# Loading the first half of batch 0's queries and keys uncast from two other queues, and taking the strided heads first

## The chip, the cores and the metric

The kernel runs on one core of a Trainium2 chip. The metric is device microseconds (us) from the start to the end of one execution; lower is better. Before the change the median of 3 runs is 304.52 us (304.48 to 304.62).

## What is computed

Attention with two kinds of local masks, then a two-layer MLP with SiLU. There are 8 batches, 8 heads, 576 positions and a head size of 64; the MLP is 512 to 2048 to 512. Heads 0 to 3 see the last 32 positions; heads 4 to 7 see every fourth of the last 128 positions.

```python
scores = scale * np.matmul(q, k.transpose(0, 1, 3, 2))
mask_plain = (rel >= 0) & (rel < window)                                   # window = 32
mask_dil = (rel >= 0) & (rel < window * dilation) & (rel % dilation == 0)  # dilation = 4
attn = softmax(np.where(masks, scores, -1e9))     # masks: plain for heads 0..3, dilated for 4..7
x = (attn @ v).transpose(0, 2, 1, 3).reshape(B * S, H * D)
h = x @ w_in
return (h * (1.0 / (1.0 + np.exp(-h)))) @ w_out
```

All inputs and the output are float32 in DRAM. The kernel works in float16 on chip.

## The kernel before

**Order of the work.** The program is scheduled by hand: the order in which the Python code calls a helper is the order in which each engine's queue gets its instructions. The MLP of batch b runs on TensorE while the attention of later batches is threaded in between its matmuls by a small plan (plan_of). Only batch 0's attention has no MLP to hide behind, so it is cut in two parts and written out by hand (lines 917 to 956): part 0 is positions 0 to 255, part 1 is positions 256 to 575. In the helpers, z = 0 means the plain heads (0 to 3) and z = 1 the strided heads (4 to 7); which = 1 is k and which = 0 is q.

**Loads.** Every load is issued by GpSimd (POOL) and converts float32 to float16 on the way. load_part(which, part) (line 133) loads all 8 heads of one part of batch 0's q or k into rows0, a view of the tile gT, which is free until the MLP starts. Part 0 puts 4 consecutive positions of each head on one of 64 partitions; the DRAM runs are 256 floats (1 KB) and land as 512 bytes. POOL's queue starts with load_part for k and q of part 0 (lines 207 and 208). Then come the identity matrix and the small mask band (lines 209 to 217), then k and q of part 1 (218, 219), the 8 loads of v for batch 0 (220), the first three quarters of w_in (222) and a piece of batch 1's k (224). The trace shows POOL's v loads waiting for earlier loads to land (the wait list puts 1.6 us on k and 1.4 us on q of part 1 ahead of line 183).

**Batch 0, part 0.** transpose0(z, which, part, copy) transposes the 4 heads of one group with TensorE into PSUM (line 302 for the strided heads, 8 transposes; line 313 for the plain heads, 16 transposes), and one engine copies the result to SBUF (line 307 to kC or qC, line 317 to kT or qT). The callers choose that engine: act is ScalarE (ACT), dve is VectorE (DVE). mask0 writes the mask into PSUM with two matmuls (line 435), scores0 adds the scores (line 390 strided, line 374 plain, 32 small matmuls each), max0 takes the row maximum (DVE, line 464), shift0 subtracts it for the strided heads (DVE, line 477), scaled scales it for the plain ones (line 483), and exps runs the exponential: one ACT instruction for the strided heads (line 563), eight with an accumulator for the plain heads (line 574). build_mask_b (line 231) makes the mask's operand on DVE from the identity and the band.

**Part 1 and the MLP.** The same steps follow for part 1, whose k and q copies stand on ACT behind part 0's exponentials. values0 and finish0 make xT, the MLP's input. warm (line 686) puts a few filler matmuls ahead of the MLP. layer1_part (line 754) multiplies w_in with part 0 of batch 0; each quarter of w_in serves 4 of the 16 column blocks (f = 0 to 3, 4 to 7, 8 to 11, 12 to 15). The plan of batch 0 puts part 1's values between them, at f = 8 and f = 10, and behind the first of these POOL's second wave of loads (loads_held, line 824).

```python
    transpose0(1, 1, 0, act)
    build_mask_b()
    transpose0(0, 1, 0, act)
    mask0(1, 0)
    transpose0(1, 0, 0, dve)
    transpose0(0, 0, 0, act)
    scores0(1, 0)
```

Of the kernel before, what the change touches and what calls it, by code (L numbers as in the profile page):

```python
# [9 lines left out]
F32 = mybir.dt.float32  # L10
# [8 lines left out]
DIL = 4  # L19
# [10 lines left out]
def kernel(  # L30
# [9 lines left out]
    nc = tc.nc  # L40
    B, H, S, D = q.shape
# [3 lines left out]
    HH = H // 2  # L45
# [8 lines left out]
    SA = NS // 2  # L54
# [6 lines left out]
    cpool = ctx.enter_context(tc.tile_pool(name="const", bufs=1))  # L61
# [62 lines left out]
    def rows0(which, part):  # L124


        t = gT[:, 4 * which : 4 * which + 4, :].rearrange("p f c -> p (f c)")
        n = H * DIL * D
        return t[0 : (SA, S - SA)[part] // DIL, part * n : part * n + n].rearrange(
            "p (h u d) -> p h u d", h=H, d=D  # L130
        )

    def load_part(which, part):

        nc.gpsimd.dma_start(  # L135
            out=rows0(which, part).rearrange("p h u d -> p h (u d)"),
            in_=bass.AP(
                (q, k)[which].tensor,
                part * SA * D,
                [[DIL * D, (SA, S - SA)[part] // DIL], [S * D, H], [1, DIL * D]],  # L140
            ),
        )

    def load_squares(b, z, which):

        for half in (0, 1):
            for x in (0, 1):  # L150
                o = half * HF + x * QB
                nc.gpsimd.dma_start(  # L152
                    out=qk[b, z, which][o : o + QB],
                    in_=bass.AP(
                        (q, k)[which].tensor,
                        (b * H + z * HH + half * HH // 2) * S * D + x * QB,
                        [[(1 + z) * D, QB], [(1 + z) * QB * D, GN[z]], [1, (QB, GW)[z]]],
                    ),
                )
# [36 lines left out]
    def load_w_out(c):  # L196
# [3 lines left out]
        )  # L200


    eps = cpool.tile([P, 1], F32, name="eps")
    nc.vector.memset(eps, EPS)
    band = cpool.tile([P, KB], F32, name="band")
    nc.vector.memset(band[0:W], 0.0)
    load_part(1, 0)
    load_part(0, 0)
    make_identity(nc, ident)
    nc.gpsimd.affine_select(  # L210
        out=band[0:W], in_=band[0:W], compare_op=ALU.is_ge, fill=NEG,
# [3 lines left out]
        out=band[0:W], in_=band[0:W], compare_op=ALU.is_ge, fill=NEG,  # L215
# [15 lines left out]
    def build_mask_b():  # L231

        nc.vector.tensor_copy(ident4, ident[0:W, None, 0:W].broadcast_to([W, 4, W]))
        nc.vector.tensor_scalar(
            mask_b.rearrange("p t (k x) -> p t k x", x=2),
            band[0:W].rearrange("p (x k) -> p k x", x=2)[:, None].broadcast_to([W, 2, W, 2]),
            1.0 / scale, None, ALU.mult,
        )
        nc.vector.memset(mask_b[:, 0].rearrange("p (k x) -> p k x", x=2)[:, :, 0], NEG / scale)
# [13 lines left out]
    def att(b):  # L253
        if b not in state:
            state[b] = {
                "qT": qTs[b % 2],
                "kT": kTs[b % 2],
                "qC": qCs[b % 2],
                "kC": kCs[b % 2],
                "vw": vws[b % 2],  # L260
                "pt": {},
                "xT": [xtp.tile([P, 2, S], F16, tag=f"xT{z}", name=f"xT_{b}_{z}") for z in (0, 1)],
            }
        return state[b]
# [26 lines left out]
    def transpose0(z, which, part, copy):  # L291

        a = att(0)
        src, t0 = rows0(which, part)[:, z * HH : z * HH + HH], part * SA
        pp = src.shape[0]
        if z:
            t = ps.tile([P, HH, 2, pp], F16, tag="ps", name=f"t{which}_0_{z}_{part}")
            for h in range(HH):  # L300
                for x in (0, 1):
                    nc.tensor.transpose(
                        t[:, h, x], src[:, h, 2 * x : 2 * x + 2].rearrange("p u d -> p (u d)"), ident[0:pp, 0:pp]
                    )
            dst, o = ((a["qC"], 0), (a["kC"], W))[which]
            o += t0 // DIL
            copy(dst[:, :, :, o : o + pp], t)
        else:
            t = ps.tile([P, 2, DIL, pp], F16, tag="ps", name=f"t{which}_0_{z}_{part}")
            for h in (0, 1):  # L310
                for x in range(DIL):
                    for i in (0, 1):
                        nc.tensor.transpose(
                            t[i * HF : i * HF + HF, h, x, :], src[:, 2 * i + h, x, :], ident[0:pp, 0:pp]
                        )
            dst = (a["qT"], a["kT"][:, :, W:])[which][:, :, t0 : t0 + pp * DIL]
            copy(dst.rearrange("d h (p u) -> d h p u", u=DIL), t.rearrange("d h u p -> d h p u"))
# [48 lines left out]
    def score(b, h, j, dst, start=True):  # L366

        if b >= DT[0]:
            score_turned(b, 0, h, 0, j, dst)
            return  # L370
        a = att(b)
        hp, o = (h % 2, h // 2 * D) if b == 0 else (h // 2, (h + h // 2) % 2 * D)
        r = slice(o, o + D)
        nc.tensor.matmul(  # L374
            dst[h * QB : h * QB + QB],
            a["qT"][r, hp, j * QB : j * QB + QB],
            keys(b, a["kT"][r, hp, j * QB : j * QB + KB]),
            start=start,
            stop=True,
            skip_group_check=not start,  # L380
        )

    def score_class(b, h, c, j, dst, start=True):

        if b >= DT[1]:
            score_turned(b, 1, h, c, j, dst)
            return
        a = att(b)
        r = slice(c % 2 * D, c % 2 * D + D)
        nc.tensor.matmul(  # L390
            dst[h * QB : h * QB + QB],
            a["qC"][r, h, c // 2, j * QB : j * QB + QB],
            keys(b, a["kC"][r, h, c // 2, j * QB : j * QB + KB]),
            start=start,
            stop=True,
            skip_group_check=not start,
        )

    def width(b, z, g):

        if b == 0:
            return 8 + g * (4 if z else 2)
        return 10 if z or g else 8
# [37 lines left out]
    def scores0(z, part):  # L441

        n = (2, 3)[part]
        w = width(0, z, part)
        sd = att(0)["s", z, part]
        if z:
            for t in range(n):
                for e in (0, 1):
                    for h in range(HH):
                        for m in (0, 1):  # L450
                            score_class(0, h, 2 * e + m, 2 * part + t, sd[:, m, e * n + t], False)
        else:
            for j in range(w):
                for h in (0, 2, 1, 3):
                    score(0, h, 8 * part + j, sd[:, j], False)
        att(0)["raw", z, part] = sd[:, :, 0 : 2 * n] if z else sd[:, 0:w]

    def max0(z, part):

        w = width(0, z, part)  # L460
        raw = att(0)["raw", z, part]
        nm = att(0)["nm", z, part] = stat.tile([P, WM], F32, tag="nm", name=f"nm_0_{z}_{part}")
        d = nm[:, 0:w].rearrange("p (m t) -> p m t", m=2) if z else nm[:, 0:w]
        nc.vector.tensor_reduce(out=d, in_=raw, axis=AX.X, op=ALU.max, negate=True)
# [135 lines left out]
    def turned(b, z, hi):  # L600

        a = att(b)
        w = width(b, z, hi)
        key = z, hi * (b == 0)
        if key not in a["pt"]:
            a["pt"][key] = ptp.tile([P, DIL * NC, KB], F16, tag="pt", name=f"pt_{b}_{z}_{hi}")
        o = width(b, z, 0) * hi if b else 0
        out = a["pt"][key][:, o : o + w].rearrange("p t c -> p (t c)")
        src = a["pn", z, hi][:, 0:w].rearrange("p t c -> p (t c)")
        if b == 0:  # L610
            out, src = out.bitcast(U32), src.bitcast(U32)
        nc.vector.transpose(out, src)  # L612
# [193 lines left out]
    dve, act = nc.vector.tensor_copy, nc.scalar.copy  # L806
# [106 lines left out]
    def turn0(z, part):  # L913
        normal(0, z, part)
        turned(0, z, part)

    transpose0(1, 1, 0, act)
    build_mask_b()
    transpose0(0, 1, 0, act)
    mask0(1, 0)  # L920
    transpose0(1, 0, 0, dve)
    transpose0(0, 0, 0, act)
    scores0(1, 0)
    max0(1, 0)
    shift0(1, 0)
    exps(0, 1, 0)
# [80 lines left out]
```

## Time and profile before

| | us |
|---|---|
| median of 3 runs | 304.52 |
| the profiled execution, its own time | 305.81 |
| its span, first to last instruction | 303.8 |
| PE (TensorE matmul) busy | 292.5, 96% of the span |
| ACT busy / DVE busy / POOL busy | 203.1 / 192.9 / 118.8 |
| mean granted TensorE clock | 0.999 |

PE is TensorE's matmul row, PEld its weight loads. The chain of waits gives PE 91% of the span, DMA 5%, POOL 1%. From about 30 us on PE hardly pauses; in the first 5.8 us it does nothing. So almost all of the time that is not PE's own lies in the first 28 us, and that is the stretch that the change touches.

In the timeline a row is: start, duration, engine, line, operation, output<-input, count, and in brackets the idle time ahead of it with what ended that idle time. In the table of windows a row is: the stretch, its length, busy time of PE, PEld, DVE, ACT and POOL with the number of instructions, the granted clock, the busy share of the 16 DMA engines (over 1 where packets overlap) and the bytes written in GB/s. Sizes given for a DMA are those that are written: a converting load reads twice as much.

The DMA list gives the two part-0 loads 256.0 KB each with 4.5 us (k) and 5.2 us (q) from issue to landing, the two part-1 loads 320.0 KB with 6.4 and 7.6 us, and the four loads of w_in 512.0 KB with a median of 8.3 us. In this kernel SyncE's queue (SP) issues only the stores of the output, the first of them at 55.3 us; ACT issues no DMA.

### The profile page before, as it was taken

The numbers are of one execution on the slowest core, as the hardware profiler recorded it, in microseconds if no ns is written. First come the engines' busy times: TensorE is split into PE (matmuls) and PEld (weight loads), VectorE is DVE, ScalarE is ACT, GpSimd is POOL, SyncE is SP. The second block draws the span as 40 slices with busy tenths as digits, with TensorE's granted clock in tenths as the row PEclk, the third lists the DMA queues.
The fourth block names the chain that finished last, engine by engine and source line by source line (L and its number), as shares of the span: only waits on it lengthen the run. The fifth ranks groups of instructions, "written<-read, shape, count | busy, mean of one in ns | idle before, by whom it ended". The sixth has DMA issues, their size and how long they took to land.

```text
span 303.8 us, 10280 instructions
## 1 busy us (share of the span) xinstructions
PE 292.5 (96%) x4395; PEld 185.9 (61%) x4395; DVE 192.9 (63%) x357; ACT 203.1 (67%) x683; POOL 118.8 (39%) x182
## 2 busy tenths in 40 slices
PE   2989999999999999999999999999999999999995
PEld 1656754677545774477644775478644775477543
DVE  1895469557997868866893768955893765800012
ACT  3677599775898659965894659976796558246200
POOL 8617326768997295336806086250000000000000
PEclk9999999999999999999999999999999999999999
DMA  8998999999999899399959199390002100210021
GB/s 100 142 196 135 193 205 124 220 154 145 132 163 198 93 71 130 113 111 40 124 72 184 38 60 131 112 121 2 2 37 106 37 2 12 95 37 0 9 97 69
DMA packets 113213, 30.47 MB, mean 100 GB/s; under 512 B 95520, under 2 KB 108688, under 8 KB 113168
## 3 DMA queue, kind: packets, MB, share of 16 engines
q0 software_dynamic: 107840, 20.38, 85.9%
q1 hardware_dynamic: 5328, 9.44, 8.7%
q8 instruction: 34, 0.56, 0.8%
q14 instruction: 11, 0.09, 0.1%
HBM read 40.75 MB, written 9.44 MB: 165 GB/s over the span
## 4 chain that ended last, share of the span: by engine, by line
PE 91%; DMA 5%; POOL 1%; issue 1%; DVE 0%; POOLq 0%
PE o L798 37%; PE h L727 37%; PE h L754 5%; PE o L774 5%; PE x L643 4%; DMA w_in<-in_moe_w_in_dram 3%; DMA gT<-in_q_dram 3%; PE s L364 2%; PE t L283 1%; POOL gT L135 1%; PE s L374 0%; PE ss L364 0%; PE s L390 0%; POOL w_in L191 0%; POOL vw L183 0%
## 5 line engine op out<-in xcount | busy, mean ns | idle before, releaser
L735 ACT ACTIVATE gT<-h 128x576 f16<-128x576 f32 x112 | 72.9, 651 | 63.6 <-PE h L727 63.4
L798 PE MATMUL o<-w_out,gT 128*128 128x512 f16 (+2 forms) x528 | 113.8, 373 | 0.0
L727 PE MATMUL h<-xT,w_in 128*128 128x288 f16 x896 | 113.2, 286 | 0.0
L727 PEld LDWEIGHTS <-w_in 128*128 128x128 f16 x896 | 86.6, 98 | 23.3
L798 PEld LDWEIGHTS <-gT 128*128 128x128 f16 x528 | 50.1, 98 | 56.0
L574 ACT ACTIVATE pe<-ms,nm 128x64 f32<-128x64 f32 x238 | 78.9, 333 | 0.1
L783 DVE COPY ob<-o 128x512 f32<-128x512 f32 (+2 forms) x35 | 23.0, 666 | 51.6 <-PE o L798 50.6
L574 ACT ACTIVATION_READ_ACCUMULATOR pe<-ms,nm 128x1 f32 x238 | 44.5, 187 | 0.0
L152 POOL DMA_DIRECT2D n<-in_k_dram x44 | 31.9, 732 | 26.5 <-DVE kC L337 25.1
L408 DVE SCALAR_TENSOR_TENSOR ms<-s,mask 128x512 f32<-128x512 f32 x28 | 19.2, 686 | 27.5 <-PE s L364 20.9
L152 POOL DMA_DIRECT2D n<-in_q_dram x44 | 31.9, 732 | 4.2 <-DMA n<-in_q_dram 3.5
L174 POOL DMA_DIRECT2D vw<-in_v_dram x32 | 18.3, 578 | 31.3 <-PE x L643 26.5
L596 DVE TENSOR_TENSOR pn<-pe,r 128x640 f16<-128x640 f32 (+2 forms) x32 | 25.3, 792 | 1.1
L183 POOL DMA_DIRECT2D vw<-in_v_dram x32 | 21.2, 667 | 11.5 <-DMA w_out<-in_moe_w_out_dram 8.4
L612 DVE STREAM_TRANSPOSE pt<-pn 128x640 f16<-128x640 f16 (+4 forms) x32 | 24.7, 772 | 1.1
L488 DVE TENSOR_REDUCE nm<-ms 128x10 f32<-128x640 f32 (+1 forms) x28 | 21.9, 786 | 0.9
L754 PE MATMUL h<-xT,w_in 128*128 128x256 f16 (+1 forms) x128 | 18.0, 291 | 1.2 <-DMA w_in<-in_moe_w_in_dram 0.9
L643 PEld LDWEIGHTS <-vw 32*64 32x64 f16 (+1 forms) x1264 | 12.8, 107 | 5.6 <-issue 5.2
L754 PEld LDWEIGHTS <-w_in 128*128 128x128 f16 x128 | 11.9, 99 | 6.0 <-DMA w_in<-in_moe_w_in_dram 2.1
L676 DVE CAST xT<-x 128x288 f16<-128x288 f32 x26 | 10.1, 450 | 8.2 <-PE x L643 8.2
L774 PE MATMUL o<-w_out,gT 128*128 128x512 f16 x64 | 14.7, 380 | 0.0
L643 PE MATMUL x<-pt,vw 32*64 32x64 f16 (+2 forms) x1264 | 14.6, 193 | 0.0
(94 smaller groups left out, 204.2 us busy)
## 6 DMA issues: line engine op xcount, KB each, us to landing
out_dram<-ob SPq DMA_DIRECT2D x35, 256.0 KB, 3.4
n<-in_k_dram POOLq DMA_DIRECT2D x24, 108.0 KB, 4.7
n<-in_q_dram POOLq DMA_DIRECT2D x24, 108.0 KB, 4.5
vw<-in_v_dram POOLq DMA_DIRECT2D x31, 80.0 KB, 3.9
vw<-in_v_dram POOLq DMA_DIRECT2D x32, 72.0 KB, 4.0
w_in<-in_moe_w_in_dram POOLq DMA_DIRECT2D x4, 512.0 KB, 8.3
w_out<-in_moe_w_out_dram POOLq DMA_DIRECT2D x4, 512.0 KB, 14.4
n<-in_k_dram POOLq DMA_DIRECT2D x20, 72.0 KB, 4.5
```

The costliest lines, as they stand in the source:

```text
L152: nc.gpsimd.dma_start(out=qk[b, z, which][o : o + QB], in_=bass.AP((q, k)[which].tensor, (b * H + z * HH + half * HH // 2) * S * D + x * Q ...
L488: nc.vector.tensor_reduce(out=nm[:, 0:w], in_=ms[:, 0:w], axis=AX.X, op=ALU.max, negate=True)
L574: nc.scalar.activation(pe[:, t, :], src[t], AF.Exp, bias=a["nm", z, hi][:, t : t + 1], scale=k, accum_out=l[:, t : t + 1],)
L596: nc.vector.tensor_tensor(pn[:, 0:w], a["pe", z, hi][:, 0:w], r[:, 0:w, None].broadcast_to([P, w, KB]), ALU.mult)
L612: nc.vector.transpose(out, src)
L643: nc.tensor.matmul(x[h // 2][h % 2 * D : h % 2 * D + D, col : col + wd], vws[b % 2][r, NB + kb * DIL + c if z else kb], turned_cols(b, pt[ ...
L727: nc.tensor.matmul(h[:, half, 0:HS], w_in16[:, c, f * P : f * P + P], xT[c // 2][:, c % 2, half * HS : half * HS + HS], start=(c == cs[0]) ...
L735: nc.scalar.activation(gT[:, f, s0 : s0 + S].rearrange("p (a c) -> p a c", a=2), h[:, :, 0:HS], AF.Silu)
L754: nc.tensor.matmul(hs[i // m][:, i % m, 0 : c1 - c0], w_in16[:, c, (f + i) * P : (f + i + 1) * P], xT[c // 2][:, c % 2, c0:c1], start=(c = ...
L774: nc.tensor.matmul(o, gT[:, f, t * P : (t + 1) * P], w_out16[:, f, :], start=(f == 0), stop=(f == NFF - 1),)
L783: copy(ob, o)
L798: nc.tensor.matmul(o[:, 0, 0:m], gT[:, f, t * P : (t + 1) * P], w_out16[:, f, cols], start=(f == 0), stop=(f == NFF - 1),)
```

## The change

The part-0 loads leave POOL. Four new float32 tiles (64 partitions, 4 heads, 256 floats: 256 KB each) take the uncast rows of k and q, one for each head group. SP issues k, ACT issues q, the strided heads' tile first on both. The conversion to float16 into rows0 becomes four engine instructions of 64x1024 elements: DVE converts k, ACT converts q. Then the hand-written order of part 0 changes: build_mask_b goes to the front; the strided k and q are converted and transposed, and their scores are taken ahead of the transposes of the plain q; the copy of the plain k goes from ACT to DVE. DVE's queue is now: mask, cast of the strided k, cast of the plain k, copy to qC, copy to kT. ACT's queue is: two DMA issues, cast of the strided q, copy to kC, cast of the plain q, copy to qT.

```diff
+    stage = {
+        (z, which): cpool.tile([SA // DIL, HH, DIL * D], F32, name=f"stage{z}{which}")
+        for z in (1, 0) for which in (1, 0)
+    }
+    def load_stage(z, which):
+        (nc.scalar, nc.sync)[which].dma_start(
+            out=stage[z, which],
+            in_=bass.AP(
+                (q, k)[which].tensor,
+                z * HH * S * D,
+                [[DIL * D, SA // DIL], [S * D, HH], [1, DIL * D]],
+            ),
+        )
+    def cast_stage(z, which, copy):
+        copy(
+            rows0(which, 0)[:, z * HH : z * HH + HH].rearrange("p h u d -> p h (u d)"), stage[z, which]
+        )
...
+    for z in (1, 0):
+        for which in (1, 0):
+            load_stage(z, which)
     eps = cpool.tile([P, 1], F32, name="eps")
...
-    load_part(1, 0)
-    load_part(0, 0)
     make_identity(nc, ident)
...
+    build_mask_b()
+    cast_stage(1, 1, dve)
+    cast_stage(1, 0, act)
     transpose0(1, 1, 0, act)
-    build_mask_b()
-    transpose0(0, 1, 0, act)
+    cast_stage(0, 1, dve)
     mask0(1, 0)
     transpose0(1, 0, 0, dve)
+    cast_stage(0, 0, act)
+    transpose0(0, 1, 0, dve)
+    scores0(1, 0)
     transpose0(0, 0, 0, act)
-    scores0(1, 0)
     max0(1, 0)
```

## The prediction, made before the change was run

> **What bounds the kernel now.** I read the chain of waits in order of time first. Up to 22 us its long pieces are transfers:
>
> ```profile
> 4.49 7.63 DMA gT<-in_q_dram
> 12.12 0.28 issue
> 12.41 0.66 POOL vw L183
> 13.07 0.75 POOL w_in L191
> 13.82 8.20 DMA w_in<-in_moe_w_in_dram
> 22.02 0.05 issue
> 22.06 1.92 PE h L754 x16
> ```
>
> Part 1's q is issued at 4.49 and lands at 12.12; that frees POOL, which issues the second quarter of w_in at 13.82; it lands at 22.02, and PE starts f = 4 to 7. From there on the chain is PE. So the change is worth what it moves that start at 22.06, or a little later one, and nothing else.
>
> Then the timeline, for the second chain that runs beside this one:
>
> ```profile
> 5.81 0.60 PE L302 MATMUL t<-ident,gT 64*128 64x64 f16 x8 [5.81 <-DMA gT<-in_k_dram]
> ...
> 8.09 0.42 DVE L307 COPY qC<-t 128x512 f16<-128x512 f16 x1 [3.89 <-PE t L302]
> ...
> 9.48 0.68 PE L374 MATMUL s<-kT,qT 64*32 64x64 f16 x32
> ...
> 10.43 0.68 DVE L464 TENSOR_REDUCE nm<-s 128x8 f32<-128x512 f32 x1
> ...
> 11.42 0.32 ACT L574 ACTIVATE pe<-s,nm 128x64 f32<-128x64 f32 x1 [0.24 <-DVE nm L483]
> ...
> 13.75 0.73 ACT L307 COPY kC<-t 128x640 f16<-128x640 f16 x1
> ...
> 19.16 2.37 PE L754 MATMUL h<-xT,w_in 128*128 128x256 f16 x16 [0.35 <-DMA w_in<-in_moe_w_in_dram]
> ```
>
> Part 0's plain heads reach ACT at 11.42; eight exponentials hold ACT until part 1's copy at 13.75; from that copy on PE works almost without a pause to 18.80 (19.16 less the 0.35 of idle) and then waits for w_in. This work chain has slack: without waits f = 0 to 3 takes 1.92 us (the 16 equal matmuls at 22.06), so PE could be at f = 4 at 18.80 + 1.92 = 20.72, 1.34 before 22.06. A shift D of the exponentials at 11.42 costs nothing until D is 1.34. Part 1's values have a little more: the DVE row that ends pt for the strided heads is at 22.18, PE uses it at 23.91.
>
> Third, the table of windows, for what a transfer gets (last column GB/s written):
>
> ```profile
> 4.00:4.50 0.50, 0.00 (x0) 0.00 (x0) 0.13 (x2) 0.00 (x0) 0.50 (x2) 1.00 1.43 195
> 19.00:19.50 0.50, 0.34 (x2) 0.28 (x3) 0.49 (x2) 0.34 (x3) 0.00 (x0) 1.00 1.24 207
> 292.00:292.10 0.10, 0.10 (x2) 0.00 (x0) 0.00 (x0) 0.00 (x0) 0.00 (x0) 1.00 1.08 410
> ```
>
> The converting loads fill SBUF at about 195 (part 0, 64 partitions) and 207 (w_in, 128 partitions); a float32 store leaves SBUF at 370 to 410.
>
> **The change part by part.**
>
> *Removed from POOL:* two issues, 0.80 + 0.69 = 1.49 us (rows at 1.25 and 2.04). The identity, the band, part 1's loads and the first v loads stand up to 1.49 earlier; the later v loads wait for part 1 to land as before, so w_in follows part 1's landing.
>
> *Added transfers.* SP and ACT come free at 0.74 (the end of the start barrier in the wait lists). Each issue takes 0.33 us on its queue (SP's row for the stores). The store issued at 291.08 moved its first byte at 291.9, its last at 292.65 and landed 2.0 us after issue, so 0.43 after its last byte. By this first bytes flow at 0.74 + 0.85 = 1.6; before they ran at full rate only from 3.8 (the window 3.5 to 4.0 has 88 GB/s). ACT's table load (1.28 us) stands behind its issues and ends before any data comes.
>
> *The rate* is the open cost: no row has a float32 load into SBUF. Bounds: 195 GB/s (nothing here has filled SBUF faster than about 210 for long) and 380 (the stores; also what 195 is on the reading side). The four tiles are 1,049 kB, twice what part 0 wrote. At 195 that is 5.4 us in place of 2.7, at 380 it is 2.8. I take 195, because the row with the same direction and the same 64 partitions is the nearest; both ends stay in the range. The Trainium skill, "SBUF — State Buffer", section "Door 1: The DMA port swizzle", speaks against the change here: partitions 0 to 63 reach only 8 of 16 ports, and a transfer into 64 partitions was measured at 196 GB/s, against 328 into 128. No run here shows it: the converting loads fit it, but they would fit a limit of the reading side as well; by the page the sum is the one at 195, by the other the one at 380.
>
> *Landings at 195.* The strided pair: 1.6 + 2.7 = 4.3, landed at 4.7 (k was there at 5.80 before, q at 7.4). The plain pair: 2.7 more, and some 0 to 0.6 for part 1's k, which now flows beside it from about 4: last byte at 7.0 to 7.6, landed at L = 7.7 (7.4 to 8.0).
>
> *Added casts.* ACT, 64x1024: 1.02 us (the 128x1024 activation at line 762). DVE: the 512-element float32 rows take 0.69, the 640-element ones 0.82, so 1.02 ns an element and 0.17 fixed, 1.22 for 1024; or, at twice that rate (the 512-element f16 copy takes 0.42), 0.69. The mask operand, SBUF to SBUF with a cast, 128 elements in 0.216, fits the double rate (the single would give 0.30); the copy of line 245, 640 in 0.81, the single. I take 0.68, since the first of these is a cast, and keep 1.22. Only one cast is on the path, that of the plain k: the strided ones end at about 5.8, under the transfer of the plain pair.
>
> *The new wait.* The cast of the plain k stands on DVE ahead of the copy to qC, and the plain k's transposes on PE ahead of the strided scores. So nothing is scored before L. From L: cast 0.68, plain k's 16 transposes 0.67, strided scores 0.45, plain q's transposes 0.64 (its ACT cast, 1.02, ended before), qT copy 0.65, plain scores 0.74, maximum 0.69, scaling and hand-over 0.3: 4.8 us. The exponentials start at L + 4.8 = 12.5 in place of 11.42: D = +1.1 (+1.6 with the slow cast). The strided heads' head start of 3 us is lost in that wait.
>
> *Moved:* build_mask_b (0.5 us of DVE) runs before data is there, free; the plain k's copy goes from ACT, 0.59, to DVE, beside PE's scores. Both cost nothing, and up to 0.6 on ACT's chain if that cover were gone.
>
> *w_in.* Its second quarter lands earlier by at most the 1.49 of POOL's queue, and later by at most 2.7 (more bytes) less 2.2 (1.6 in place of 3.8) = 0.5, if all loads share one 195. I take the middle, some 0.4 earlier: 21.6.
>
> **Sum.** PE reaches f = 4 at the later of 20.72 + 1.1 = 21.8 (22.3 with the slow cast) and 21.6 (20.5 to 22.5). Against 22.06 that is -0.2, with -0.5 to +0.5 from the bounds. PE is the chain from there, so the end moves by as much. The profiled execution took 305.81 (span 303.8 and 2.0 around it), 1.29 over the median; the shift is put on the median: 304.52 - 0.2 = 304.3.
>
> **Rivals.**
>
> *Full gain.* The float32 loads run at 380: strided pair landed at 3.4, plain pair at about 5.1; D = 5.1 + 4.8 - 11.42 = -1.5; PE at f = 4 by 19.2 for its own work, w_in 1.5 earlier by POOL's queue: 20.5. The end moves by -1.5 (-1.0 to -1.9): 303.0. For it: reads ran at 390 and a store at 410, so the engines can. Against it: no fill of SBUF over some 210.
>
> *The plain pair is late.* Part 1's loads on POOL's queue take a larger share than assumed. The place is the plain k's cast in DVE's queue, with everything behind it. It decides from D = 1.34, which is L = 11.42 + 1.34 - 4.8 = 8.0 (7.4 with the slow cast). If the two kinds of queue share evenly from 4, L is about 9: D = 2.4, PE at f = 4 at 23.1, +1.0 to the end. Halfway, at 8.5, it is 1.9, 22.6 and +0.6. I give it 305.3 (304.7 to 305.8).
> For it: 8.0 is near my 7.7. Against: POOL's first bytes come 0.9 us or more after its issue, and half-size packets take less of a turn.
>
> *DVE and POOL in each other's way.* Three equal copies of line 244 took 184, 187 and 428 ns while POOL was issuing loads. The casts run while POOL issues without a pause. At 0.24 (that row's excess) to 0.75 (one POOL issue) on the plain k's cast D is 1.3 to 1.9: up to +0.5, 304.8. The Trainium skill, "SBUF — State Buffer", section "Who interferes with whom", has the rule: a DVE copy or cast in a two-port mode and a GpSimd instruction exclude each other. The 428 ns agree with it, but are one row.
>
> **Chances.** Forecast 0.40, full gain 0.34, late plain pair 0.18, DVE and POOL 0.08. About 0.2% (0.6 us) is what a measurement of this kernel tells from no change. The forecast's own range, 304.0 to 305.0, is nearly all within that; I give 0.04 to its lower tail and 0.03 above, and split the last case. Faster 0.38, same 0.37, slower 0.25. The range takes in the full gain and most of the late pair: 302.8 to 305.5.
>
> **What would show it.** In the changed kernel's profile: windows from 1.5 to 7 at about 195 GB/s (forecast) or 350 and more (full gain); DVE's cast of the plain k at about 7.7 or at 5; that cast at 0.68, 1.22, or longer beside POOL; the first exponential of line 574 near 12.5 or 10; the first idle of PE at line 754 ended by w_in or by the chain. The forecast is wrong if the rate is not near 195, if first bytes do not come by 1.6, or if the landing of part 1, and with it w_in, moves by more than a microsecond either way.

## The result, and the profile after

The changed kernel takes 306.66 us in the median (306.11 to 307.37) against 304.48 (304.42 to 304.62) for the kernel before: a ratio of 1.0078 with a 95% interval of 1.0063 to 1.0093. It is slower by about 2.2 us; the prediction was 304.3 with a range up to 305.5. The profiled execution took 307.37 with a span of 305.5, against 305.81 and 303.8. Line numbers below are those of the changed kernel: 162 is the casts, 325 and 336 the transposes (strided, plain), 413 and 397 the scores, 597 the plain exponentials, 777 the first MLP layer, 1029 the kernel's end.

The chain of waits, in order of time (start, duration, what). Ahead of it stand only SP's first issue (0.75 to 1.47):

```profile
1.53 7.66 DMA stage<-in_k_dram
9.21 0.70 DVE gT L162
...
9.95 0.63 PE t L336 x9
...
11.56 0.59 ACT qT L340
...
12.20 0.71 PE s L397 x25
...
12.94 0.70 DVE nm L487
...
14.15 2.48 ACT pe L597 x16
...
21.29 4.80 PE h L777 x32
```

Before, this chain went through part 1's q on POOL's queue and then w_in. Both are gone from it in this execution (in another one w_in still held PE: see "beside" below). It now begins with SP's second load, the plain k, issued at 1.53 and landed at 9.21, and runs through every step of part 0 that the prediction counted from L. No wait of PE is ended by w_in here: its second quarter, issued at 14.05, was there 8.2 later, and PE came to it after that.

The timeline of the same execution, for the four landings and for what follows:

```profile
5.05 1.04 ACT L162 CAST gT<-stage 64x1024 f16<-64x1024 f32 x1 [1.62 <-DMA stage<-in_q_dram]
6.39 0.69 DVE L162 CAST gT<-stage 64x1024 f16<-64x1024 f32 x1 [4.19 <-DMA stage<-in_k_dram]
...
9.21 0.69 DVE L162 CAST gT<-stage 64x1024 f16<-64x1024 f32 x1 [2.13 <-DMA stage<-in_k_dram]
...
21.08 5.01 PE L777 MATMUL h<-xT,w_in 128*128 128x256 f16 x32
26.02 0.70 PE L666 MATMUL x<-pt,vw 32*64 32x32 f16 x64
```

The strided q is there at 5.05, the strided k at 6.39, the plain k at 9.21. By the chain above, the exponentials of the plain heads start at 14.15; before they started at 11.42. PE begins w_in at 21.08 (19.16 before) and needs 5.01 for 32 equal matmuls; 16 of them took 1.92 at best before. In the trace the first 13 of these matmuls follow each other at 0.21 us and the rest at 0.11; before, only the first 5 were that slow. Part 1's values stand at 26.02, 2.1 later than before (23.91).

The table of windows (stretch, length, busy times, clock, DMA share, GB/s written):

```profile
3.50:4.00 0.50, 0.00 (x0) 0.00 (x0) 0.00 (x0) 0.00 (x0) 0.50 (x2) 1.00 1.15 303
4.00:4.50 0.50, 0.00 (x0) 0.00 (x0) 0.00 (x0) 0.00 (x0) 0.50 (x2) 1.00 1.12 209
...
6.50:7.00 0.50, 0.00 (x0) 0.00 (x0) 0.50 (x1) 0.00 (x0) 0.50 (x1) 1.00 1.16 196
```

The float32 loads into 64 partitions reach 281 (3.0 to 3.5) and 303, and then settle at 196 to 209. The forecast's 195 was right for all but that microsecond, whose cause is not shown; the 380 of the first rival was not.

The DMA queues (packets, MB, share) in the microsecond from 5 to 6. q10 is ACT's queue (q), q1 is SP's (k), q0 POOL's:

```profile
q10 hardware_dynamic: 168, 0.16, 90.4%
q1 hardware_dynamic: 45, 0.04, 22.7%
```

SP and ACT do not share each moment evenly: here 168 to 45, and from 6 to 7 it is 33 to 166. By the packets, q10 carried the strided q from 2.24 to 4.06, q1 the strided k from 3.23 to 5.34, q10 the plain q from 4.10 to 6.62, q1 the plain k from 5.35 to 8.04. At each change both flow for about a microsecond; between the changes one queue has nearly all the bytes: turn by turn, nearly a whole transfer at a time. POOL's k of part 1, issued at 1.78, moved its first byte at 6.63 (before: issued at 1.25, first byte of the queue at 2.76) and landed at 10.66 (10.13 before). The Trainium skill, "DMA: Bandwidth & Descriptors", section "Queues, rings and completion order", states that an engine goes round its queues and drains a whole packet, 9 to 17 descriptors as a rule, before it switches. The trace agrees for SP and ACT: each of these transfers is 272 records, 17 for each of 16 engines if they share evenly, so one turn would be one transfer. By the same rule POOL's queue should have had its turn earlier than 6.63; that part the trace does not bear out.

**Where the 1.7 us of span went.** Against before, in the timelines, part 1's values stand 2.1 later; the next columns of w_in 2.0 (24.62 to 26.66); w_out's first matmuls 1.0 (41.37 to 42.37); and from there the shift stays at 1.00 to the last matmuls (283.41 to 284.41 in the chains). So 1.1 of the shift is given back between 26 and 42. The other 0.7 lies behind the last copy of the output: from its end to the end of the span are 2.75 us before and 3.46 after. SyncE's last waits (what, us, times, longest), before and then after:

```profile
SPq L1002 <- DMA out_dram<-ob: 0.9, 2, 0.6
...
SPq L1002 <- SPq L1002: 0.4, 1, 0.4
```

```profile
SPq L1029 <- DMA out_dram<-ob: 1.2, 1, 1.2
...
SPq L1029 <- PEq L1029: 0.7, 2, 0.5
```

Before, the 0.9 us on the stores are two waits of up to 0.6; after, one of 1.2. At the end SP waits for the transfers' semaphores one after another. With four hardware transfers more, the last store's semaphore has moved from the sixth to the second place in that row, so SP still has the rest of the row to walk when the store lands.

The two profiled executions are not equally typical: 305.81 is 1.29 over the median that the prediction started from, 307.37 is 0.71 over the median of its kernel. So the two profiles lie 1.6 apart where the medians lie 2.2 apart.

### The profile page after: what moved, and what is told of

It is laid out like the page before. It is cut to its first block, busy times and chain, and to the rows that moved or that the text cites. A ratio compares the mean times of both kernels' runs of the same rounds, so it can differ in the third digit from the quotient of the medians.

```text
span 305.5 us, 10290 instructions
## 1 busy us (share of the span) xinstructions
PE 292.5 (96%) x4395; PEld 186.6 (61%) x4395; DVE 194.6 (64%) x360; ACT 204.5 (67%) x684; POOL 118.1 (39%) x180
## 4 chain that ended last, share of the span: by engine, by line
PE 94%; DMA 3%; ACT 1%; DVE 1%; issue 0%; SPq 0%; ACTq 0%
PE o L821 37%; PE h L750 36%; PE h L777 6%; PE o L797 5%; PE x L666 4%; DMA stage<-in_k_dram 3%; PE s L387 2%; PE s L397 1%; ACT pe L597 1%; PE t L306 1%; PE s L413 1%; PE t L336 0%; PE ss L387 0%; PE h L709 0%; SPq L151 0%
## 5 line engine op out<-in xcount | busy, mean ns | idle before, releaser
L196 POOL DMA_DIRECT2D vw<-in_v_dram x32 | 18.4, 587 | 31.9 <-PE x L666 27.1
L205 POOL DMA_DIRECT2D vw<-in_v_dram x32 | 21.8, 697 | 12.6 <-DMA w_out<-in_moe_w_out_dram 7.6
```

## The experiments

Ratios are to the kernel before on the same chip. "Exponentials" is the start of the plain heads' first one, "tail" the time from the end of the last copy of ob to the end of the span.

| kernel | median us | ratio, 95% | exponentials | tail |
|---|---|---|---|---|
| changed, again | 307.24 | 1.0079 (1.0055 to 1.0102) | 13.83 | 3.43 |
| changed, beside | 307.20 | 1.0077 (1.0056 to 1.0099) | 13.31 | 3.47 |
| order only | 304.98 | 1.0011 (0.9994 to 1.0027) | 11.44 | 2.77 |
| q on the upper 64 partitions | 306.49 | 1.0059 (1.0039 to 1.0079) | 13.23 | 3.4 |
| SP issues all four | 308.99 | 1.0148 (1.0120 to 1.0176) | 16.09 | 3.35 |
| plain casts later | 308.74 | 1.0126 (1.0096 to 1.0157) | 15.11 | 3.4 |
| all 128 partitions | 304.81 | 1.0002 (0.9985 to 1.0020) | 10.97 | 3.4 |
| 12 filler matmuls | 306.80 | 1.0064 (1.0041 to 1.0086) | 13.09 | 3.4 |
| before, four small loads | 305.05 | 1.0002 (0.9985 to 1.0019) | 11.44 | 3.37 |
| queues swapped | 306.18 | 1.0043 (1.0022 to 1.0063) | 12.95 | 3.4 |
| changed, four small loads | 306.40 | 1.0061 (1.0042 to 1.0081) | 13.89 | 2.7 |
| 128 partitions, four small loads | 303.82 | 0.9975 (0.9955 to 0.9994) | 11.02 | 2.76 |

**The changed kernel again**, unaltered:

> The changed kernel once more, unaltered. In its first profile the four float32 loads moved from 2.2 to 8.0 us, the plain k landed at 9.2 and the exponentials of the plain heads started at 14.15 in place of 11.42. Theory (late plain pair): the landing order and times repeat within 0.3 us, and the time is again near 306.7, some 2.2 over the kernel before. Rival (turns between the queues are drawn anew in each execution, which would also explain the spread of 306.1 to 307.4): the plain k lands at another time by over 0.5 us in this profile.

The loss repeats. So does its place: the strided k at 6.14, the plain k at 9.10, the tail of 3.43. A third execution, "beside" below, has the same loss with another order of landing.

**The new order alone.** The loads stay on POOL and convert, as before; only the order of part 0 is the changed one.

```diff
-    for z in (1, 0):
-        for which in (1, 0):
-            load_stage(z, which)
...
+    load_part(1, 0)
+    load_part(0, 0)
...
-    cast_stage(1, 1, dve)
-    cast_stage(1, 0, act)
...
-    cast_stage(0, 1, dve)
...
-    cast_stage(0, 0, act)
```

> Part 0 is loaded by POOL as in the kernel before, converted on the way; nothing is cast by an engine; only the new order of the transposes and scores is kept, with the plain k's copy on DVE. Theory (the loads cost, the order does not): within 0.3 us of the kernel before, 304.2 to 304.8, since k lands at 5.8 and q at 7.4 whatever the order. Rival (the order costs, since plain k's transposes stand ahead of the strided scores and the plain q's behind them): exponentials of the plain heads later than 11.42 by 0.5 to 1 us, and the time up to 0.5 over.

Measured: 1.0011, an interval that holds 1, and the exponentials at 11.44 (11.42 before). The new order costs nothing that can be measured by itself. The loss is in the loads.

**k and q on different halves of the partitions**, the same transfers otherwise; k stays on partitions 0 to 63, q and its float16 rows go to 64 to 127.

```diff
-        return t[0 : (SA, S - SA)[part] // DIL, part * n : part * n + n].rearrange(
+        p0 = HF if which == 0 and part == 0 else 0
+        return t[p0 : p0 + (SA, S - SA)[part] // DIL, part * n : part * n + n].rearrange(
```

> As the changed kernel, but q of part 0 is loaded into, cast on and transposed from partitions 64 to 127 in place of 0 to 63; k stays on 0 to 63. Bytes, DMAs, queues and engine instructions are the same in number and size. Theory (how many partitions are reached limits the fill, 205 GB/s for 64): k and q now fill at the same time, 350 GB/s or more between 3 and 6 us, the plain k lands at about 7 in place of 9.2 and the time falls by 1.5 us or more against the changed kernel. Rival (the two hardware queues are served one DMA at a time, or each float32 DMA has its own limit): the rate stays near 205, the plain k lands within 0.5 us of 9.2 and the time stays within 0.5 us of the changed kernel.

```profile
4.00:4.50 0.50, 0.00 (x0) 0.00 (x0) 0.00 (x0) 0.00 (x0) 0.50 (x2) 1.00 1.14 238
```

In this row of its table of windows, and in the next two (229, 240), the rate is about 235 in place of 205, far from 350. The two halves would add up only if k and q flowed at once, and they take turns: at any moment mostly one half is being written. The plain k landed at 8.50. Both expectations missed by size, and since the two halves are seldom filled at once, this run cannot tell the partitions from another limit; the next one can.

**All 128 partitions.** Two positions on each partition in place of four on 64: the same bytes, 512-byte packets, casts of 128x512, half as many transposes.

```diff
-        (z, which): cpool.tile([SA // DIL, HH, DIL * D], F32, name=f"stage{z}{which}")
+        (z, which): cpool.tile([P, HH, 2 * D], F32, name=f"stage{z}{which}")
...
-                [[DIL * D, SA // DIL], [S * D, HH], [1, DIL * D]],
+                [[2 * D, P], [S * D, HH], [1, 2 * D]],
...
+                nc.tensor.transpose(t[:, h], src[:, h].rearrange("p u d -> p (u d)"), ident)
+            copy(dst[:, :, :, o : o + HF], t.rearrange("d h (m x) -> d h x m", x=2))
```

> As the changed kernel, but a partition holds 2 consecutive positions of part 0 in place of 4, so the four float32 tiles and rows0 fill all 128 partitions: packets of 512 bytes, casts of 128x512 (DVE 0.42, ACT 0.6), half as many transposes of twice the size. The same bytes in the same four DMAs. Theory (64 partitions limit the fill): 350 GB/s or more from 3 us on, the last float32 byte at about 6 in place of 8, the plain k at about 7 in place of 9.2, the plain exponentials at about 11.3, and the time within 0.5 us of the kernel before. Rival (each queue's DMAs are served whole and in turn at some 205 GB/s whatever the partitions): the last byte at 7.5 or later, plain exponentials near 13.5, time at least 1 us over the kernel before.

Its windows, and then its timeline:

```profile
4.00:4.50 0.50, 0.00 (x0) 0.00 (x0) 0.12 (x1) 0.00 (x0) 0.50 (x2) 1.00 1.15 345
4.50:5.00 0.50, 0.14 (x2) 0.14 (x3) 0.30 (x1) 0.16 (x1) 0.50 (x1) 1.00 1.18 329
```

```profile
6.05 0.48 DVE L164 CAST gT<-stage 128x512 f16<-128x512 f32 x1 [1.25 <-DMA stage<-in_k_dram]
...
20.62 1.92 PE L795 MATMUL h<-xT,w_in 128*128 128x256 f16 x16 [0.83 <-DMA w_in<-in_moe_w_in_dram]
```

The rate now holds at 329 to 345, the plain k is there at 6.05, 3 us sooner, and the exponentials start at 10.97, 0.45 ahead of the kernel before and 4.92 behind L, as in the changed kernel (4.94). So the shorter casts and transposes that come with this layout are not what helps; the earlier landing is. The bytes read are the same, so reading is not what held the loads at 205. It is the one change of layout that took the loss away (1.0078 to 1.0002). The rule that the prediction cited from the Trainium skill, "SBUF — State Buffer", section "Door 1: The DMA port swizzle" (196 GB/s into 64 partitions, 328 into 128, measured with transfers of 1 MiB), agrees with the settled rates of these traces, about 205 and 340, but not with the 281 and 303 between 3 and 4 us. What is next is w_in: PE waits 0.83 for its second quarter.

**SP issues all four**, so that ACT's queue is left out:

```diff
-        (nc.scalar, nc.sync)[which].dma_start(
+        nc.sync.dma_start(
```

> As the changed kernel, but SP issues all four float32 loads (strided k, strided q, plain k, plain q) and ACT none. Theory (one stream of bytes at about 205 GB/s, whoever issues): the same bytes in the same time, k ahead of q within a pair now, so the plain k lands some 0.5 us or more earlier and the plain q later than 8; the time is within 0.7 us of the changed kernel. Rival (two queues disturb each other): the four loads end a microsecond or more earlier than 8.0. Apart from that: the profile of the changed kernel ends 3.5 us after its last copy, that of the kernel before 2.75; if the use of ACT as a DMA queue makes that, it goes back to 2.75 here, and the time falls by some 0.7.

The queues from 5 to 6 us:

```profile
q0 software_dynamic: 153, 0.08, 70.3%
q1 hardware_dynamic: 83, 0.08, 36.2%
```

With one hardware queue POOL's moves its first byte at 4.13 and has half of the bytes from 5 to 6. The strided k came at 4.48, the plain k at 9.86 and the plain q at 11.96; 1.0148. Both expectations missed: the plain k came later, not earlier, and the last of the loads came at 11.96. The tail stayed at 3.35, so it is not ACT's use as a queue that makes it. So the second hardware queue is what keeps POOL's waiting, and the four tiles gain by it.

**The queues swapped**: ACT issues k, SP issues q.

```diff
-        (nc.scalar, nc.sync)[which].dma_start(
+        (nc.sync, nc.scalar)[which].dma_start(
```

> The changed kernel with the two queues swapped: ScalarE's queue carries both k tiles, SyncE's both q tiles; nothing else differs. Theory (the two queues are served in turn, a whole transfer each, ScalarE's first): k and q change places, so the strided k lands at about 5.0 us (6.1 to 6.4 in the changed kernel), the plain k at 8.2 (9.1 to 9.2), the plain q at 9.2. The strided scores stand about 1 us earlier, near 9.6. The plain heads then wait for q: 9.2 + cast 1.04 + transposes 0.64 + copy 0.65 + scores 0.74 + maximum and hand-over 1.0 = 13.3, against 13.8 to 14.15. Time 306.3 to 306.8. Rival (both tiles of a pair share the rate, and k is late because its queue or its issue is slow): k lands no earlier on the other queue, the exponentials stay at 13.8 or later, time 307 or more.

```profile
4.82 0.73 DVE L162 CAST gT<-stage 64x1024 f16<-64x1024 f32 x1 [2.62 <-DMA stage<-in_k_dram]
7.33 0.69 DVE L162 CAST gT<-stage 64x1024 f16<-64x1024 f32 x1 [1.78 <-DMA stage<-in_k_dram]
```

In this timeline k lands at 4.82 and 7.33, strided scores stand at 8.64 in place of 10.51, and the plain q becomes the last (cast at 8.64). The exponentials start at 12.95; 306.18. That is as the theory of turns expected, and sooner. One doubt stays: in the profiled execution of the changed kernel "beside", unaltered, SP was served first as well (k at 4.98 and 7.74). Which queue has the first turn is not fixed by the engine that issues.

**The plain casts later**: behind the strided scores, maximum and shift, so that nothing of the strided heads waits for the plain k.

```diff
-    cast_stage(0, 1, dve)
...
-    cast_stage(0, 0, act)
-    transpose0(0, 1, 0, dve)
...
     shift0(1, 0)
+    cast_stage(0, 1, dve)
+    cast_stage(0, 0, act)
+    transpose0(0, 1, 0, dve)
```

> As the changed kernel, but the plain heads' casts and transposes stand behind the strided heads' scores, maximum and shift, so nothing of the strided heads waits for the plain k any more. Theory (what costs is that the plain k lands at 9.2 and all scores stand behind it): the strided scores come near 9.2 in place of 10.5; behind the landing there are then left cast 0.7, transposes 0.65, copy 0.7, scores 0.7, maximum 0.7, scaling 0.3, so the plain exponentials start near 13.2 in place of 14.15 and the time falls by 0.6 to 1.0 us against the changed kernel, still over the kernel before. Rival (the order of DVE's queue does not matter, part 1's loads landing late set the end): plain exponentials earlier, the time within 0.3 us of the changed kernel.

```profile
10.30 0.69 DVE L500 TENSOR_TENSOR ms<-s,nm 128x512 f32<-128x512 f32 x1
10.91 0.67 DVE L162 CAST gT<-stage 64x1024 f16<-64x1024 f32 x1
```

The expectation failed, with the opposite sign. The strided scores did start earlier, at 9.04, but the plain k, which had landed about 8.5, now waits on DVE behind their maximum and shift until 10.91. The exponentials move to 15.11. Not all of the 308.74 is this: in the profiled execution PE also stands idle for 1.70 us in the middle of part 0's values (to 20.76), ended by nothing that the profile shows. The order in the changed kernel is not at fault: with a late plain k, what stands ahead of its cast is on the path.

**Filler matmuls** ahead of the first transposes, since PE took 0.157 us in the mean for each of the first 32 matmuls with w_in and 0.12 later:

```diff
+    fill = big.tile([P, 512], F32, tag="big", name="fill")
+    warm(fill, 12)
     build_mask_b()
     cast_stage(1, 1, dve)
```

> As the changed kernel, with 12 filler matmuls of 512 columns on TensorE ahead of the first transposes, in time that it spends waiting. In the changed kernel's profile the first 32 w_in matmuls take 0.150 us each, and 0.12 after that; in the kernel before only the first 16 are slow (0.148) and the next 16 take 0.12. Theory (TensorE speeds up only after a stretch of dense work, and the changed kernel reaches it later): with the fillers the small matmuls of part 0 and the first w_in matmuls run at the fast rate, 0.12 each, and the time falls by 0.7 us or more against the changed kernel. Rival (the slow w_in matmuls are slowed by the transfers beside them): they stay at 0.15, and the time stays within 0.3 us.

Its timeline of PE and its windows (9 to 12 us):

```profile
6.84 0.40 PE L325 MATMUL t<-ident,gT 64*128 64x64 f16 x8 [0.46 <-DVE gT L162]
...
10.05 0.64 PE L336 MATMUL t<-ident,gT 64*64 64x64 f16 x16 [0.98 <-ACT gT L162]
...
19.99 1.92 PE L777 MATMUL h<-xT,w_in 128*128 128x256 f16 x16
```

```profile
9.00:12.00 3.00, 1.88 (x64) 1.16 (x52) 1.73 (x3) 2.11 (x3) 0.66 (x1) 0.56 1.45 193
```

The same eight transposes take 0.40 behind fillers and 0.60 without. From 9 to 12 the granted clock is 0.56, and the plain transposes take the 0.64 that they take in the changed kernel, where the same column says 1.00. So a clock column of 1.00 in the first microseconds does not mean full speed here. The Trainium skill, "TensorE: Matmul & The Clock Gate", section "Part 1: The HAM clock gate (the "warmup" mystery)", has an idle array at 1.2 GHz and a busy one at 2.4, switched by a window of about 3.4 us that runs freely. The trace agrees: the 0.56 is near a half, and the 0.21 and 0.11 us between the matmuls with w_in have the ratio of two; the eight transposes, with 0.60 to 0.40, gain less. The first 16 matmuls with w_in now take 1.92, but PE then waits 1.54 (to 23.46), and the time is not clearly below that of the changed kernel (1.0064 and 1.0079). And "beside", with no filler, also had 1.91, while "again" took 5.49 for the first 32 and the kernel before with four small loads 5.14. So the slow 5.01 varies with the execution and is not made by the change; the fillers settle nothing about it.

**Four small loads in the kernel before.** SP loads 2 KB four times into a tile that nothing reads: the number of hardware transfers of the changed kernel, with nothing else of it.

```diff
+    extra = cpool.tile([P, 4, 4], F32, name="extra")
+    for i in range(4):
+        nc.sync.dma_start(out=extra[:, i], in_=q[0, 0, i * P : i * P + P, 0:4])
```

> The kernel before, with four loads of 2 KB each issued by SP at the start into a tile that nothing reads. Theory (the end of the program, 0.65 to 0.7 us longer in all kernels with the float32 loads, comes from the number of DMAs on SP and ACT, by which the semaphore of the last store moves in the row of waits at the end): span minus the end of the last copy is 3.4 in place of 2.75, and the time is 0.4 to 0.9 us over the kernel before although nothing else is changed. Rival (the longer end comes from the float32 data or from where it is written): the end stays at 2.75, and the time within 0.3 us.

The tail becomes 3.37 from 2.75, so four transfers more are enough to make it. The median is no different (1.0002), where 0.6 us would be 1.002, just outside the interval.

**Four small loads in two other kernels**: in the one with 128 partitions, and in the changed one, with the unaltered changed kernel beside it on the same chip. Both put the count of transfers to eight more than before.

> The kernel with two positions per partition in all 128 partitions, and beside it four 2 KB loads by SyncE into a tile that nothing reads, behind its two stage loads. Theory (the extra time behind the last copy comes from the place that the last store's semaphore has in SyncE's row of waits at the end, and eight transfers more in place of four put it back): from the end of the last copy of ob to the end of the span 2.75 us in place of 3.4, and the time 0.6 below that of two positions per partition: 304.2 (303.9 to 304.6). Rival (that tail is paid in the profiled execution alone, as four small loads beside the kernel before seemed to say): the tail is 2.75, the time stays at 304.8 within 0.3. Second rival (any transfer more makes the tail longer): 3.4 or more, time 304.8 to 305.2.

> The changed kernel with four 2 KB loads by SyncE, behind its stage loads, into a tile that nothing reads. Theory (the place of the last store's semaphore in SyncE's row of waits at the end costs real time): from the end of the last copy of ob to the end of the span 2.75 us in place of 3.4, and 0.6 less than the changed kernel on the same chip: about 306.3 where that has 306.9. The front, up to the plain exponentials at 13.8 to 14.2, is unchanged. Rival (that tail shows in the profiled execution but does not move the time): 2.75, and the same time as the changed kernel within 0.3. Second rival (the small loads take their turn ahead of the stage tiles): the exponentials later than 14.2, and the time above that of the changed kernel.

> The changed kernel, unaltered, on the same chip as the one with four small loads, for the comparison alone: 306.7 to 307.2, the plain exponentials at 13.8 to 14.2, the tail 3.4. Both theories expect the same of it; by the first the kernel with the four loads lies 0.6 below it, by the rival within 0.3 of it.

SyncE's last waits in the kernel with 128 partitions and small loads:

```profile
SPq L1050 <- DMA out_dram<-ob: 0.9, 2, 0.7
...
SPq L1050 <- PEq L1050: 0.7, 2, 0.5
```

The wait for the store is again split in two with 0.7 the longest, and the tail is back at 2.76 and 2.7, though more transfers are issued: their place in the row counts, not their number. The medians follow twice: 304.81 to 303.82 (ratios 1.0002 and 0.9975, different chips), and 307.20 to 306.40 on one chip (1.0077 and 1.0061). Each pair of intervals overlaps, and the kernel before with four loads did not follow. That the tail depends on the row is shown; that it costs the median 0.6 is likely, not settled. The kernel with 128 partitions and small loads is below the kernel before too, if only by a quarter of a percent: 0.9975 (0.9955 to 0.9994).

**What "beside" shows besides.** In this execution of the unaltered changed kernel k had the first turn. From its timelines of ACT and of PE:

```profile
9.14 1.04 ACT L162 CAST gT<-stage 64x1024 f16<-64x1024 f32 x1 [1.31 <-DMA stage<-in_q_dram]
```

```profile
23.36 1.92 PE L777 MATMUL h<-xT,w_in 128*128 128x256 f16 x16 [1.31 <-DMA w_in<-in_moe_w_in_dram]
```

The plain k was there at 7.74, the forecast's L, and still the exponentials started at 13.31, because the plain q came last, at 9.14. And PE, which needed w_in's second quarter by 22.05, had it at 23.36: a landing of 9.3 us in place of 8.2, issued at 14.0. So two paths lead to the late f = 4, the last of the plain pair and w_in, and which of them binds differs between executions; an earlier k alone does not win the loss back. In the run with swapped queues PE waits for w_in too, until 23.34.

## Why the prediction was wrong, point by point

- **The rate** (195 taken, 380 the other end): right, 196 to 209.
- **The landing of the plain pair**, L = 7.7 (7.4 to 8.0): this step failed; it was 9.21. Half of the 1.5 stands before the last byte and half behind it. First bytes were to flow at 1.6; they flowed at 2.24. An issue of such a load takes 0.7 to 0.8 on its queue and not the 0.33 of a store, which is 0.4 of that; the rest came between the end of the issue and the first byte. The last float32 byte came at 8.04 (7.0 to 7.6 forecast). And from last byte to use it took 1.17 (0.65 with 128 partitions, 1.74 with SP alone), not the 0.43 of the store's row: the store was the wrong row for a load in both. In "beside" the plain k kept the forecast (7.74) and the plain q did not (9.14): it is the later of the pair that counts, where the prediction had the cast of q end before.
- **The shares.** I let part 1's k flow beside the plain pair from 4 and cost up to 0.6. In fact POOL's queue got nothing until 6.63, and k stood a turn behind q. So POOL's head start, 1.96 us at part 1's first issue (3.74 to 1.78), was gone when part 1 landed: k at 10.66 (10.13 before), q at 12.33 (12.12 before). The queues' turns were not in the prediction at all.
- **w_in**, 0.4 earlier at 21.6: wrong by its sign. With part 1 no earlier, its first issue went from 13.06 to 13.28. In the execution "beside" PE waits for it until 23.36. With 128 partitions, where part 1 does come earlier, PE has it at 20.62.
- **From L to the exponentials**, 4.8: right, 4.94 (9.21 to 14.15); the cast 0.68 forecast and 0.69 measured. D was therefore 2.73, not 1.1, almost wholly by L.
- **The slack of 1.34**: right in kind. At D = 2.73 it would leave 1.39 at f = 4; part 1's values moved by 2.1, as the first 32 matmuls took 5.01 where 2 x 1.92 was assumed, less 0.45 by which PE came to them sooner than 18.80 + 2.73.
- **"The end moves by as much"**: failed in the other direction. Of 2.1 at 26 us, 1.0 was left at 42. What gave it back are small idle times of PE that stand in the timeline of before (at 26.99, 28.67, 34.4 and 40) and not in that of after. They differ between executions of one kernel too: "beside" had the exponentials 0.84 sooner than the first profile and ended with the same shift. Some 0.6 of what the profiles lack against the medians goes with the choice of executions (above), and part of this give-back may too. What makes the idle times was not tried and stays open.
- **The tail**, 0.7 in the profile: not thought of. The prediction counted the four new transfers at the front and nothing at the end.
- **The rivals.** "The plain pair is late" is what happened, beyond its own case: with L about 9 it gave D = 2.4 and +1.0, and the front did end +1.0 later in the profile. Its price of 305.3 lacked the tail; it also used a middle L of 8.5 for its range. DVE and POOL in each other's way did not decide here: the plain k's cast at 9.21 took 0.69, but POOL issued nothing then (7.36 to 10.96). DVE's cast of the strided k ran beside POOL's issues and took 0.69 here, 0.73 with swapped queues, 0.78 with fillers and 0.88 in "plain casts later": up to 0.2 more, and done before the plain pair landed. The full gain fell with the rate.

What is shown, then: the loss comes from the loads and not from the order (order only), and from how they fill 64 partitions (128 partitions take it away). That the two queues' turns put one half of each pair behind the other is shown by the packets and fits the swap. About 0.6 to 0.8 of the 2.2 is likely the row of waits at the end.

## What to carry to other kernels

A load that converts on the way writes half the bytes of an uncast one; moving the cast to an engine doubles the bytes that enter SBUF, so ask first how fast that side fills, and use all 128 partitions for a transfer on the critical path. Take issue and landing times from a load of the same kind, not from a store, and look at which queue has its turn before counting on a head start. Count transfers at the end of the kernel too: a few added at the start can change which semaphore is waited for last.

## What the hardware showed that was not expected

- Two hardware queues took turns of a whole 256 KB transfer, and POOL's queue moved nothing beside them for 4.85 us after its issue (1.78 to 6.63; 1.51 in the kernel before); beside one hardware queue its first byte came at 4.13.
- Into 64 partitions, the microsecond from 3 to 4 ran at 281 and 303 GB/s, and from then on about 205; into 128, 329 to 345 from 3.5 to 5.0.
- From the last byte to the first use, the load of the plain k took 1.17 us (0.65 to 1.74 in other runs); the store of before took 0.43 from last byte to landing.
- Transposes ran at 0.60 or 0.40 for the same eight, and matmuls with w_in at 0.21 or 0.11 apart, while the clock column said 1.00 in both.
- Four tiny loads, with nothing else changed, made the stretch from the last copy to the end 0.6 us longer; beside the four tiles, the same four loads made it 0.7 shorter again.
